# New assignment of heads to groups, column-half loads of wq and wk, and a new instruction order in a transformer block on one core

## The chip, the cores and the metric

The kernel runs on one core of a Trainium2 chip. The metric is the device time of one execution in microseconds, of which the median of several runs is taken. Five engines run their own instruction streams and meet at semaphores: TensorE (PE in the profile, its weight loads PEld), VectorE (DVE), ScalarE (ACT), GpSimd (POOL) and SyncE (SP). SP here does nothing but issue DMAs.

## The reference

x is 2048 tokens of 640 numbers (bf16). The block computes

```
h   = x + A(layernorm(x))          # attention with a memory, 32 heads of 20
out = h + B(layernorm(h))          # MLP, 640 -> 1728 -> 640, silu
```

A splits the 2048 tokens into four segments of 512. In each segment and for each head it computes

```
p     = softmax(q k^T * scale + causal mask);   a_dot = p v
a_mem = (phi(q) M) / (phi(q) z + 1e-6)          # M, z: from the segments before
o     = g * a_mem + (1 - g) * a_dot             # g = sigmoid(beta) of the head
M    += phi(k)^T v;   z += sum phi(k)           # phi(t) = t + 1 if t > 0, else exp(t)
```

and multiplies the concatenated heads with wo. wq, wk, wv and wo are 640 by 640, w1 is 640 by 1728 and w2 1728 by 640.

## The kernel before, in words

**Tiles and stages.** Each 128-token block goes through layer norm (task `n1_st` statistics, `n1_rs` reciprocal root on POOL, `n1_ap` application), is transposed and becomes the moving operand of the projections. The first four blocks are transposed on TensorE against an identity (`n1_tp`, L791) and copied out (`n1_te`, L800); later ones by a DMA (`n1_tr`, L806). Statistics of blocks 1 and 2 can run on ACT (L744 to L748) or on DVE (L753, L756).

**Heads.** 32 heads of 20 numbers form eight groups of four. q and k of a segment live in five chunks of 128 partitions. In a chunk each of four row blocks of 32 partitions holds 20 numbers of one head of a whole group, and in its last 12 partitions a part of a head of one of the remaining three groups: chunks 0 to 2 hold 12 numbers of the heads of groups 5 to 7, chunks 3 and 4 the other 8 of groups 5 and 6 and 4 plus 4 of group 7. `rearr` (L687 to L717) copies the raw weights, which lie in `wraw` (a part of the tile sT), into that order: tasks `re_wq0`, `re_wq0h` (chunk 0 in two parts by rows), `re_wq1` to `re_wq4`, and the same for wk. Groups 5 to 7 get their q and k in one piece through 12 small SBUF-to-SBUF DMAs for each segment, `vt<segment><0..11>` (L908), issued by SP.

**One tick** is a head group in a segment: scores q k (`qk`, L946, four row tiles of the array), exp on ACT (`e`, L959, two pieces for each of the score blocks a, b and, for every second group, e), causal mask on POOL (`mk`, L971), p v (`av`, L994, four column tiles), scaling (`oe`), transposition back and memory part (`td`, `tm`), division and sum (`nm`, `ad`). Ticks 0 to 7 belong to segment 0, 8 to 15 to segment 1 and so on. After a segment come the memory sums (`kt` transposes phi(k) by DMA, `mz`, L1112, multiplies it with v), wo, the second layer norm and the MLP (`h1`, `th`, `s`, `h2`, then `o` and the store `out`).

**Order.** Nothing is scheduled at run time. `ORDER` (L362) is a list of 1462 task names made beforehand, with each task's buffer slots and, where there is a choice, the engine (/A ACT, /D DVE, /G POOL, /S SP). `/C` has a full 128-column matmul issued as four matmuls on column tiles of 32 (L549 instead of L548). The emission follows the list, so each engine executes its tasks in list order, and a wait holds up all that stands behind it on that engine. PE thus changes between three tilings of its array: full (L548, L620, L791), four row tiles (L946) and four column tiles (L549, L994, L1112, L1198).

**Loads at the start.** SP issues, in this order, x block 0, block 1, blocks 2 and 3 together, wq in two parts by rows of the input dimension (480 and 320 KB), wk likewise, wv, beta, x blocks 4 to 7, then parts of w1. The two parts of wq follow `KS`, the two row ranges:

```
KS = [range(0, 3), range(3, 5)]
load_w(f"{n_}{z}", wraw[:, w_, k0_:k1_, :], cw(src)[:, k0_:k1_, :], ...)      # 1280-byte runs
```

In the list the first projections are `pr000x`, `pr000y`, `pr001x`, `pr001y` (chunk 0, q and k, two 256-token halves each), then `pr011`, and after it the first scores `qk0a0`.

Of the kernel before, what the change touches and what calls it, by code (L numbers as in the profile page):

```python
# [234 lines left out]
class Graph:  # L235
# [52 lines left out]
    def schedule(self):  # L288
# [3 lines left out]
        for row in ORDER:  # L292
# [53 lines left out]
GRP_BLK = [[(0, 0)], [(1, 2)], [(2, 4)], [(3, 6)], [(4, 9)],  # L346
           [(0, 1), (3, 7)], [(1, 3), (4, 10)], [(2, 5), (3, 8), (4, 11)]]
# [25 lines left out]
pr041.0:2 e1b0:6 pr041.1 x8/S:8,9,10,11 v03.1 e1b2 qe041/D:0 ex031:0 qk2a0:4,6 n1_tr4 mm5 mk0e pa041:2 n1_rs6 n1_ap6:2
n1_tr6 n1_ap7:3 ex041:2 mzc10 mm2 mk0b pr040.0:3 e2a0:3 mta3 pr040.1 pr030.0:2 ve03/D e2a2 qk2b0:4,0 e2b0:0 vt06
pr030.1/C qe040/D pa031:0 av0:3 pb021 mk1a qe030/D mm1 n1_tr7 vt05 oe0/D:0 qk2e0:6,4 vt010 mk1b av1:2 e2b2 epsg1 mk2b
pb041 mk2a td0/C:3 e2e2:5 e2e0 oe1/D:1 qk3a0:4,0 nm0:3,0 vt07 e3a2:6 v10.0:2 td1:6 nm1:2 vt011 e3a0 v10.1 ve10/D:1
qk3b0:0,6 e3b2:4 e3b0 mm7 n1_st9:2 mk2e av2:3 mk3a oe2/D:1 qk4a0:6,4 e4a2:3 v11.0/C:2 e4a0 v11.1/C qk4b0:0,4 td2/C:6
epsg0 ve11/D pb031 mk3b nm2:2 mtb3 av3:7 e4b0:1 vt01 e4b2 vt02 n1_rs9 oe3/D:0 mzc1 n1_st10:7 vt08 n1_st8:1 vt04
qk4e0:2,0 mk4a pr100.0/C:4 e4e2:4 pr100.1/C qe100/D:0 pa100:0 qk5a0:0,6 pr110.0/C:5 pr110.1/C e4e0 qe110/D:0 e5a0:5
w_wo/S:0 qk5b0:2,0 pr120.0/C:4 pr120.1/C qe120/D:0 mk4b e5a2 mk4e av4:5 oe4/D:1 mk5a kt02:0 pa120:0 e5b2:2 qk6a0:0,6  # L380
n1_rs8 td3/C:4 n1_ap8:0 nm3:0 e5b0 mk5b v12.0:2 v12.1 kt04:4 ve12/D e6a0:1 ex120:0 e6a2 w_w2_3/S td4:1 ex100:1 mz01:0
mz00 mm8 mz04 mz02 kt03:1 n1_rs10 n1_ap10:3 mz03 ma0/D:0 qk6b0:4,2 e6b2:0 e6b0 mk6b nm4:3 pr101.0:7 pr101.1 qk6e0:0,2
e6e2:6 qe101/D av5:6 pr111.0/C:7 pr111.1/C e6e0 qk7a0:4,2 mk6e w_w2_0/S mk6a e7a0:4 e7a2 n1_tr8:1 mk7a oe5/D:0 qe111/D
td5:6 pr130.0/C:0 pr130.1/C nm5:1 n1_tr10 qk7b0:6,4 e7b2:5 e7b0 mk7b n1_ap9:0 qe130/D:0 n1_st11:7 v13.0:1 mm3 v13.1/C
ve13/D ex101:2 n1_rs11 av6:0 qk8a0:3,6 e8a0:3 pa101:0 e8a2 pr140.0:5 pr140.1/C av7:4 oe6/D:1 mzc3 qk8b0:0,2 w_w1_4/S
td6/C:6 e8b0:2 w_w1_3/S n1_tr9 mzc5 pb101 kt10:1 qe140/D:0 oe7/D:0 mk8a nm6:2 pr131.0/C:7 td7/C:4 nm7:1 mzc7 mzc4
ot0:0 qk8e0:5,0 pr131.1/C ot1 n1_ap11:1 mm0 qe131/D pr121.0:4 pr121.1 pa130:0 pa110:0 ot2 qe121/D vt19:0 pa131:1 mzc0
# [935 lines left out]
```

## Time and profile before

| | us |
|---|---|
| median of 3 runs (297.17 to 298.87) | 297.37 |
| the profiled execution, its own time | 295.65 |
| its span in the trace | 293.9 |
| PE busy | 282.0 |
| DVE busy | 218.6 |
| ACT busy | 216.5 |
| POOL busy | 148.1 |

The profiled execution took 295.65 us, 1.75 us more than the span between its first and last recorded instruction, and 1.72 us less than the median of the three runs. Busy time of PE is modelled from pipelined matmuls, so a busy PE is not PE at its peak. In timelines the columns are start, duration, engine, line, operation, output and input, count, and in brackets the idle time before with what ended it. SPq marks the time that SP's DMA queue took to issue.

### The profile page before, as it was taken

Reading aid. Unit: us, or ns where it says so; the run is one execution under the profiler, and the core shown is the slowest. Engines: PE = TensorE matmul, PEld = TensorE weight load, DVE = VectorE, ACT = ScalarE, POOL = GpSimd, SP = SyncE. Lnnn points to the kernel's source line nnn. Section 1 sums busy time; section 2 is a strip of 40 time slices with the busy share of each in tenths; the row PEclk is TensorE's granted clock in tenths of the full one; section 3 lists DMA queues with packets and bytes.
Section 4 is the critical chain, followed back from the end, with each engine's and each line's share of the span. In section 5 each row is a group of like instructions: output and inputs, shape, how many; then the busy total and the mean of one; then the engine's idle time right before and its main releaser. Section 6 shows DMA issues by size and latency. Waiting matters only on the chain.

```text
span 293.9 us, 10138 instructions
## 1 busy us (share of the span) xinstructions
PE 282.0 (96%) x4365; PEld 159.8 (54%) x4365; DVE 218.6 (74%) x456; ACT 216.5 (74%) x281; POOL 148.1 (50%) x294
## 2 busy tenths in 40 slices
PE   6899889999999999999999899999999999999996
PEld 5454435445644445566654554656664657754574
DVE  3999888899997678798899835877746776635613
ACT  7699999999999899977789857979979640005400
POOL 6759675686947545746748432348638321300000
PEclk9999999999999999999999999999999999999999
DMA  7947869635464200453543402403320031450003
GB/s 212 342 120 186 113 176 186 167 69 108 87 80 113 73 2 3 53 99 70 91 122 92 93 2 21 81 2 57 73 25 2 2 70 22 91 156 0 3 0 112
DMA packets 48604, 24.83 MB, mean 84 GB/s; under 512 B 38896, under 2 KB 47472, under 8 KB 48560
## 3 DMA queue, kind: packets, MB, share of 16 engines
q1 hardware_dynamic: 48560, 24.19, 38.1%
q8 instruction: 34, 0.56, 0.8%
q14 instruction: 10, 0.08, 0.1%
HBM read 10.41 MB, written 2.62 MB: 44 GB/s over the span
## 4 chain that ended last, share of the span: by engine, by line
PE 83%; DVE 7%; ACT 6%; DMA 1%; issue 1%; POOL 0%; SPq 0%; ACTq 0%; DVEq 0%
PE ps_all L548 49%; PE ps_all L549 20%; PE ps_all L946 8%; ACT PT L959 5%; PE ps_all L994 5%; DMA x_tok<-in_A_x_dram 1%; PE ps_all L1198 1%; DVE xn_rot L781 1%; DVE oTs L1010 1%; DVE phiQ L890 1%; DVE stt L753 1%; PE ps_all L1112 1%; DVE Vx L843 1%; DVE otok L1046 1%; DVE QK L877 0%
## 5 line engine op out<-in xcount | busy, mean ns | idle before, releaser
L959 ACT ACTIVATE PT<-ps_all 128x1024 bf16<-128x1024 f32 x160 | 154.1, 1027 | 16.2 <-PE ps_all L946 15.1
L971 POOL TENSOR_SCALAR_AFFINE_SELECT PT<-PT 128x512 bf16<-128x512 bf16 x128 | 82.8, 651 | 63.9 <-ACT PT L959 60.5
L1211 ACT ACTIVATE th<-ps_all 128x512 f32<-128x512 f32 (+1 forms) x56 | 31.7, 589 | 38.1 <-PE ps_all L548 23.7
L1217 DVE SCALAR_TENSOR_TENSOR sT<-th,ps_all 128x512 bf16<-128x512 f32 (+1 forms) x56 | 36.0, 661 | 17.0 <-ACT th L1211 16.4
L548 PE MATMUL ps_all<-w_sb,sT 128*128 128x320 bf16 x324 | 46.3, 299 | 0.1
L548 PE MATMUL ps_all<-tT,w_sb 128*128 128x512 bf16 x178 | 41.4, 380 | 0.0
L548 PEld LDWEIGHTS ps_all<-w_sb,sT 128*128 128x128 bf16 x324 | 31.0, 98 | 13.2 <-issue 0.6
L753 DVE BATCH_NORM_STATS2 stt<-x_tok 128x6 f32<-128x320 bf16 x62 | 27.1, 478 | 3.8 <-DMA x_tok<-in_A_x_dram 3.6
L1072 POOL TENSOR_TENSOR otok<-on 128x320 bf16<-128x320 bf16 x24 | 19.7, 824 | 17.5 <-DVE on L1064 17.5
L1254 DVE SCALAR_TENSOR_TENSOR x_tok<-ps_all,x_tok 128x640 bf16<-128x640 f32 (+1 forms) x17 | 13.3, 784 | 17.9 <-PE ps_all L548 13.1
L548 PEld LDWEIGHTS ps_all<-tT,w_sb 128*128 128x128 bf16 x178 | 16.5, 98 | 18.7 <-issue 0.6
L877 DVE CAST QK<-ps_all 128x512 bf16<-128x512 f32 x25 | 17.1, 685 | 8.6 <-PE ps_all L548 4.7
L1010 DVE TENSOR_SCALAR oTs<-ps_all,lsc 128x512 bf16<-128x512 f32 x26 | 19.3, 741 | 2.6 <-PE ps_all L994 2.2
L549 PE MATMUL ps_all<-tT,w_sb 128*32 128x512 bf16 x328 | 20.5, 380 | 0.0
L1064 DVE TENSOR_TENSOR on<-ps_all,rd 128x640 bf16<-128x640 f32 x24 | 19.8, 824 | 0.8
L765 POOL TENSOR_TENSOR rst<-rst,eps_c 128x1 f32<-128x1 f32 x32 | 18.3, 573 | 2.5
L549 PE MATMUL ps_all<-w_sb,sT 128*32 128x320 bf16 x496 | 18.8, 300 | 0.0
L781 DVE TENSOR_SCALAR xn_rot<-x_tok,mvt,rst 128x640 bf16<-128x640 bf16 x31 | 16.1, 534 | 3.3 <-POOL rst L765 2.8
L548 PE MATMUL ps_all<-tT,wkr 128*128 128x512 bf16 (+1 forms) x77 | 18.4, 367 | 0.0
L548 PE MATMUL ps_all<-wv_sb,tT 128*128 128x320 bf16 x115 | 18.0, 300 | 0.5 <-ACT PT L959 0.3
L763 POOL TENSOR_TENSOR rst<-mvt,eps_c 128x1 f32<-128x1 f32 x32 | 6.7, 209 | 22.5 <-DVE mvt L756 21.8
L994 PE MATMUL ps_all<-PT,Vx 128*32 128x512 bf16 (+3 forms) x384 | 17.4, 301 | 0.0
(111 smaller groups left out, 403.1 us busy)
## 6 DMA issues: line engine op xcount, KB each, us to landing
out_dram<-x_tok SPq DMA_DIRECT2D x15, 160.0 KB, 1.9
w_sb<-in_B_w_dram SPq DMA_DIRECT2D x5, 432.0 KB, 4.1
x_tok<-in_A_x_dram SPq DMA_DIRECT2D x3, 640.0 KB, 4.4
w_sb<-in_B_w_dram SPq DMA_DIRECT2D x3, 480.0 KB, 4.0
QKV<-QK SPq DMA_DIRECT2D x12, 72.0 KB
wv_sb<-in_A_wv_dram SPq DMA_DIRECT2D x1, 800.0 KB, 8.2
wo_sb<-in_A_wo_dram SPq DMA_DIRECT2D x1, 800.0 KB, 5.3
w_sb<-in_B_w_dram SPq DMA_DIRECT2D x1, 640.0 KB, 6.0
```

The lines of the kernel that those rows point to most:

```text
L548: return [lambda e: e.matmul(out, lhsT=lhsT, rhs=rhs, start=start, stop=stop)]
L549: return [lambda e, p=p: e.matmul(out[p:p + 32, :], lhsT=lhsT[:, p:p + 32], rhs=rhs, start=start, stop=stop, tile_position=(0, p)) for p i ...
L753: T.add(DV, lambda e, hh=hh: e.bn_stats(out=stt[:, s, 6 * hh:6 * hh + 6], in_=xb[:, 320 * hh:320 * hh + 320]), reads=R((xa, xsub)), writes ...
L946: fns.append(lambda e, j=j, o=o, r=r, q0=q0, q1=q1, qa=qa, ka=ka: e.matmul(ps_all[:, o:o + q1 - q0], lhsT=ka[32 * r:32 * r + DH, 128 * j:1 ...
L959: T.add(AC, lambda e: e.activation(out=pt[:, pta.slot, q0:q0 + 2, 0:width], in_=sc3[:, b0:b0 + 2, 0:width], func=ACT.Exp, scale=SCALE), re ...
L971: fns.append(lambda e, v=v: e.affine_select(out=v, in_=v, pattern=[[0, 4], [1, 128]], compare_op=ALU.is_ge, fill=0.0, base=0, channel_mult ...
L994: fns.append(lambda e, j=j, r=r, h=h, pa=pa, pt=pt, co=co, q0=q0, ji=ji: e.matmul(bank(po)[32 * r:32 * r + 32, q0:hi], lhsT=vtile(vx)[:, j ...
L1010: f = lambda e: e.tensor_scalar(out=o, in0=i_, scalar1=lsc[:, g:g + 1], scalar2=None, op0=ALU.mult)
L1064: T.add(DV, lambda e: e.tensor_tensor(out=on[:, ona.slot, :, :].rearrange("p b (x e) -> p b x e", e=DH), in0=v[:, :, :, 0:DH], in1=r2.unsq ...
L1072: T.add(PO, lambda e: e.tensor_tensor(out=o_dst, in0=on[:, ona.slot, 0, :].rearrange("p (i x) -> p i x", i=4), in1=on[:, ona.slot, 1, :].r ...
L1211: T.add(AC, lambda e: e.activation(out=th[:, tha.slot, lo:hi], in_=bank(ps)[:, lo:hi], func=ACT.Tanh, scale=0.5), reads=R((ps, [0])), writ ...
L1217: T.add(DV, lambda e: e.scalar_tensor_tensor(out=sT[:, f, lo:hi], in0=th[:, tha.slot, lo:hi], scalar=1.0, in1=bank(ps)[:, lo:hi], op0=ALU. ...
```

## The change

It has four parts.

1. **Heads.** A table `SG = [0, 2, 6, 4, 5, 1, 3, 7]` says which four consecutive heads make up each group. Chunk 0 now holds heads of the weights' blocks 0 and 1, chunk 1 of blocks 2 and 3, which all lie in columns 0 to 319. Chunk 2 needs columns 320 to 639 alone, chunks 3 and 4 both halves.
2. **Loads.** wq and wk are loaded in column halves of 400 KB, in the order q left, k left, q right, k right.
3. **Memory sums.** Chunks 3 and 4 swap their parts of groups 5 and 6 (`GRP_BLK`, `blk_type`). `mz` of chunk 4 now is one run of three heads with a constant stride, 16 matmuls of 63 columns, instead of 16 of 42 and 16 of 21 columns.
4. **A new list**: other order, slots and engines for the same 1462 names.

```
+SG = [0, 2, 6, 4, 5, 1, 3, 7]
...
-        for z, ks in enumerate(KS):
-            k0_, k1_ = ks[0], ks[-1] + 1
-            load_w(f"{n_}{z}", wraw[:, w_, k0_:k1_, :], cw(src)[:, k0_:k1_, :], -94 + w_, 6.58, [(sT0, [f"{n_}{z}"])], "fix",
+        for z in range(2):
+            load_w(f"{n_}{z}", wraw[:, w_, :, 320 * z:320 * z + 320], cw(src)[:, :, 320 * z:320 * z + 320], -94 + 2 * z + w_, 6.58,
...
+        four = lambda g: hv[:, :, 4 * SG[g]:4 * SG[g] + 4, :]
...
+            parts = sorted({SG[g] // 4 for g in [c] + ([5 + c] if c < 3 else [2 + c, 7])})
...
-                rr, ww = [(sT0, ["qk"[wi] + q for q in ("01" if c else "01"[z])])], [(W[k], [c + 5 * z])]
+                rr, ww = [(sT0, [f"{'qk'[wi]}{q}" for q in parts])], [(W[k], [c + 5 * z])]
...
-                heads = [(4 * c, 16, 2)] if c < 3 else [(12, 8, 3)] if c == 3 else [(16, 8, 2), (28, 1, 1)]
+                heads = [(4 * SG[c], 4, 2)] if c < 3 else [(4, 12, 3)] if c == 3 else [(12, 8, 3)]
```

The list up to the second half of the first score block, before and after:

```
-epsc:0 iota halfc zpad warm:0 x0:0 mt2 n1_st0:4 mt3 mt0 mt1 mta1 mtb1 vpad1 x1:1 n1_st1/A:1,2 x2:2,3 w_q0:0 w_q1 w_k0
-vpad0 fill25:0 n1_rs0 n1_ap0/A:1 sel n1_tp0:2 fill5:7 n1_te0/A:1 n1_st2/D:5,3 mta0 n1_rs1 n1_st3:0 n1_rs2 w_k1 w_wv:0
-n1_rs3 re_wk4/G:0 mtb0 mm4 n1_ap1 n1_tp1:0 n1_ap2 n1_tp2:4 n1_ap3:0 n1_tp3:2 re_wq0/D:0 n1_te1/A pr000x.0:6 re_wq0h/D
-re_wk2/G pr000x.1 re_wk0/D re_wq2/D n1_te2/A n1_te3/A pr001x.0:5 qe000x/D:0 re_wk0h/D pr000y.0:4 re_wq3/G beta
-pr001y.0:0 x4/S:4,5,6,7 pr000y.1 qe000y/A w_w1_1/S:0 mta2 mtb2 mm10 pr001y.1 re_wk1/D re_wq1/D qe001y/A pr001x.1
-pr011.0:2 pr011.1 re_wk3/D qe001x/A re_wq4/G qk0a0:0,3 ex001:0 pa001:0 pb001 kt00:2 pr021.0:7 pr021.1 e0a2:4 qe011/D:0
...
+iota:0 halfc mt3 x0:0 zpad fill25:0 sel n1_st0:0 mt1 epsc mta1 mtb1 warm:0 x1:1 n1_st1/D:6,1 x2:2,3 n1_st2/A:4,3
+w_q0:0 w_k0 n1_rs0 n1_rs1 n1_ap0/D:2 n1_st3:7 w_q1 w_k1 n1_ap1 n1_tp0:2 fill5:7 n1_rs2 n1_ap2 n1_te0/A:0 re_wq0/A:0
+n1_tp1:5 re_wq0h/D n1_rs3 w_wv:0 n1_tp2:0 n1_ap3:0 n1_tp3:2 n1_te1/A pr000x.0:4 re_wk0/G:0 re_wk0h/G n1_te3/D n1_te2/A
+re_wq2/A pr000x.1 qe000x/D:0 re_wq1/A re_wk1/D beta mm5 pr001x.0:6 pr001x.1 pr001y.0:1 x4/S:4,5,6,7 pr000y.0:4
+pr000y.1 pr001y.1 re_wk2/D pr011.0:7 pr021.0:3 qe000y/A qe001y/A qe001x/A ex001:2 qk0a0:4,1 pa001:2 pb001 pr021.1
+pr011.1 vpad0 qe021/D:0 pr010.0:6 pr010.1 qe011/D:0 pa011:1 e0a2:1 n1_st4:1 kt00:4 x8/S:8,9,10,11 qk0b0:2,0 e0a0
```

Counted over the whole program, PE has 4365 matmuls before and 4356 after, with the same number of columns, and changes the tiling of its array 173 times before and 177 times after. After the start, PE's order in segment 0 is close to the old one (`qk0b0`, `pr020`, `v00`, `qk0e0`, `v01`, `v02`, `qk1a0`, `pr031`, and so on). Of the choices of engine in segment 0, `qe020` goes from ACT to DVE, `re_wq0`, `re_wq1` and `re_wq2` from DVE to ACT, and one load of w1 (`w_w1_3`) is issued from ACT. In SP's order of segment 0, `n1_tr6` (the last of the four block transposes that segment 1's projections need) stood ahead of all but three of the twelve `vt` issues before; after, it stands behind the last of them.

More of the change, by code (lines that the diff above doesn't have):

```diff
@@ L373 @@
[L373 to L387, printed above, removed]
@@ L673, in build @@
             channel_multiplier=-1), reads=[f"mt{k}"], writes=[f"mt{k}"], prio=1)
[L674 to L675 removed]
+    blk_type = {0: 0, 2: 0, 4: 0, 7: 0, 10: 0, 1: 1, 3: 1, 5: 1, 6: 2, 9: 2, 8: 3, 11: 3}
+    blk_head = {m: 4 * SG[g] for g, bl in enumerate(GRP_BLK) for _, m in bl}
     for k in range(12):
@@ L1007, in e_ot @@
                 if eng == AC:
-                    f = lambda e: e.activation(out=o, in_=i_, func=ACT.Identity, scale=lsc[:, g:g + 1])
+                    f = lambda e: e.activation(out=o, in_=i_, func=ACT.Identity, scale=lsc[:, SG[g]:SG[g] + 1])
                 else:
-                    f = lambda e: e.tensor_scalar(out=o, in0=i_, scalar1=lsc[:, g:g + 1], scalar2=None, op0=ALU.mult)
+                    f = lambda e: e.tensor_scalar(out=o, in0=i_, scalar1=lsc[:, SG[g]:SG[g] + 1], scalar2=None, op0=ALU.mult)
                 T.add(eng, f, reads=R((po, [0]), (C, ["lsc"])), writes=R((ots, [0])))
```

203 lines of the change are left out of this document (108 added, 95 removed).

## Prediction

> **What bounds the kernel now.** I read the page first (shares of the chain that ended last), then windows of ten microseconds, then the timeline of the start, since the change names the start.
>
> ```profile
> PE   6899889999999999999999899999999999999996
> ACT  7699999999999899977789857979979640005400
> PE 83%; DVE 7%; ACT 6%; DMA 1%; issue 1%; POOL 0%; SPq 0%; ACTq 0%; DVEq 0%
> ...
> 0.00:10.00 10.00, 6.40 (x50) 4.55 (x50) 4.89 (x18) 7.22 (x11) 6.51 (x27) 1.00 0.81 257
> ...
> 30.00:40.00 10.00, 8.05 (x186) 4.31 (x178) 7.91 (x19) 9.86 (x12) 6.57 (x14) 1.00 0.65 78
> 40.00:50.00 10.00, 9.02 (x243) 4.78 (x236) 9.34 (x20) 9.44 (x12) 6.88 (x14) 1.00 1.10 249
> 50.00:60.00 10.00, 9.96 (x169) 4.38 (x165) 8.78 (x19) 9.90 (x11) 6.02 (x11) 1.00 0.59 127
> ```
>
> In the windows the columns after the length are PE, PEld, DVE, ACT and POOL. PE carries the chain. It is idle for 10.00 - 6.40 = 3.6 us of the first ten (fillers included in busy), 1.95 us at 30 to 40 and 0.98 us at 40 to 50, where ACT is busy for 9.86 and 9.44 of ten. Of PE's 293.9 - 282.0 = 11.9 us of idle time, 6.5 lie in these three windows. So the start counts in full, segment 0 (to about 60 us) is bound by ACT and PE together, and the rest by PE.
>
> The timeline of the start:
>
> ```profile
> 2.19 1.00 SPq L584 DMA_DIRECT2D sT<-in_A_wq_dram  x2
> 3.24 1.00 SPq L584 DMA_DIRECT2D sT<-in_A_wk_dram  x2
> 3.59 0.74 ACT L744 ACTIVATE xn_rot<-x_tok 128x640 bf16<-128x640 bf16 x1 [0.23 <-DMA x_tok<-in_A_x_dram]
> 5.42 0.19 ACT L748 ACTIVATION_READ_ACCUMULATOR xn_rot<-x_tok,stt 128x1 f32 x1
> 5.88 0.88 DVE L753 BATCH_NORM_STATS2 stt<-x_tok 128x6 f32<-128x320 bf16 x2 [1.56 <-DMA x_tok<-in_A_x_dram]
> 7.07 0.70 ACT L800 ACTIVATE tT<-ps_all 128x640 bf16<-128x640 f32 x1 [0.55 <-PE ps_all L791]
> 7.08 0.19 POOL L763 TENSOR_TENSOR rst<-mvt,eps_c 128x1 f32<-128x1 f32 x1 [0.56 <-DVE mvt L756]
> 7.35 0.55 POOL L765 TENSOR_TENSOR rst<-rst,eps_c 128x1 f32<-128x1 f32 x1
> 9.22 0.45 DVE L781 TENSOR_SCALAR xn_rot<-x_tok,mvt,rst 128x640 bf16<-128x640 bf16 x1 [0.51 <-POOL rst L765]
> 9.73 0.45 PE L791 MATMUL ps_all<-ident,xn_rot 128*128 128x128 bf16 x5 [0.51 <-DVE xn_rot L781]
> 10.08 0.71 PE L548 MATMUL ps_all<-tT,wqr 128*128 128x256 bf16 x5
> 10.45 1.06 POOL L711 COPY wkr<-sT 128x400 bf16<-128x400 bf16 x3 [1.33 <-DMA sT<-in_A_wk_dram]
> 11.86 1.68 PE L548 MATMUL ps_all<-tT,wkr 128*128 128x256 bf16 x9
> 12.06 0.94 ACT L876 ACTIVATE w_sb<-ps_all 128x256 bf16<-128x256 f32 x3 [1.14 <-PE ps_all L548]
> 13.03 0.63 ACT L883 ACTIVATE ex<-w_sb 128x512 bf16<-128x512 bf16 x1
> 13.47 0.39 PE L946 MATMUL ps_all<-w_sb 20*128 20x512 bf16 x4
> 13.80 1.25 PE L548 MATMUL ps_all<-tT,wkr 128*128 128x512 bf16 x5
> 13.92 1.94 ACT L959 ACTIVATE PT<-ps_all 128x1024 bf16<-128x1024 f32 x2 [0.26 <-PE ps_all L946]
> 18.39 0.60 ACT L876 ACTIVATE w_sb<-ps_all 128x512 bf16<-128x512 f32 x1
> ```
>
> What the reader is to see: only POOL ever waits for the weights (until 10.45, for wk). PE's first projection at 10.08 follows block 3's transpose (9.73), its normalization (9.22), the reciprocal roots on POOL, and the x load that landed at 5.88. The weights are not the gate; the layer norm of blocks 2 and 3 is.
>
> **The change, part by part.** *Layer norm at the start.* The x loads keep their place, so blocks 2 and 3 land at 5.88 again. The new list puts block 2's statistics on ACT. Block 1's took 3.59 to 5.42 + 0.19 = 5.61 there, 2.02 us, so block 2's end at 5.88 + 2.02 = 7.90. The root tasks stand on POOL in the order 2, 3; each takes 7.08 to 7.35 + 0.55, 0.82 us. So block 2's root is done at about 8.75 and block 3's, though its statistics are early, at 9.6. Block 3's normalization (0.45) ends at 10.05 and its transpose (0.45) at 10.55. The first projection starts at about 10.55 instead of 10.08: **+0.45 us** on PE.
>
> *First scores.* The 20 half projections of chunk 0 took 10.08 to about 12.3 (11.86 + 1.68, less 1.25 for the five 512-column ones in that row): 2.2 us, so they now end at 12.75. Ahead of the first scores now stand six 512-column matmuls (`pr011.0`, `pr021.0`) at 0.24 each (1.25 / 5), as against five: 14.2 instead of 13.47. The first exp comes about 0.75 later, at 14.65. ACT itself is ready by then: from 7.90 it does three copies (0.70 each), the half `re_wq0` and two whole rearrangements, which no row shows on ACT. By the 0.63 and 0.94 / 3 rows for 512 and 256 numbers I put 0.55 and 0.85 for them; that gives 12.3, then 0.94 and 0.63, 14.1. The slack is half a microsecond.
>
> *ACT after that.* `qe020` (0.60, the row at 18.39) goes to DVE, which loses five rearrangements at the start. A load of w1 is issued from ACT, and no row shows that; on SP the two issues of a weight part take 1.00 together, so between 0 and 0.5 for one. ACT's stream is thus between 0.75 - 0.60 = +0.15 and +0.65 late, PE's 0.45 late. I take **+0.45** for both, with ends of 0 (the list is otherwise close to the old one, and idle time of PE at 30 to 50 can take it up) and +1.0.
>
> *The loads.* Half of each weight is enough for chunk 0. wk's last part was issued at about 3.75 and landed at about 10.4 (POOL's row). The bytes ahead of each part are known: 655 KB of x, then 410 KB each. If time goes by bytes, k left lands at about 8, q right at 9.2 and k right at 10.4. Needed: q left at 8.6, k left at 9.6 (POOL), q right at 10.6 (ACT), k right at about 12.3 (DVE). All are hidden, so the loads gain **0**: POOL's wait of 1.33 goes, and what is late next on the path is the root of block 3. If the cover were gone, each microsecond would delay the first scores by one.
>
> The runs shrink from 1280 to 640 bytes, 1280 packets more. Their price is bounded by these rows, of 3 to 11 us and of 292 to 294 us:
>
> ```profile
> DMA packets 2155, 2.64 MB, mean 330 GB/s; under 512 B 94, under 2 KB 2155, under 8 KB 2155
> q1 hardware_dynamic: 2155, 2.64, 102.2%
> ...
> DMA packets 288, 0.16 MB, mean 82 GB/s; under 512 B 32, under 2 KB 288, under 8 KB 288
> q1 hardware_dynamic: 288, 0.16, 26.4%
> ```
>
> At the start a packet of about 1225 bytes takes 16 x 8 x 1.022 / 2155 = 61 ns. At the end, stores of 640-byte rows take 16 x 2 x 0.264 / 288 = 29 ns. So half a packet costs about half, and I take 0; the upper end is a full 61 ns each, rival 3. The Trainium skill, "DMA: Bandwidth & Descriptors", Why small descriptors are slow, gives a packet about 3 cycles beside its 32-byte beats, by which 640 bytes cost 46 cycles for what took 43: as an estimate k right would land some 0.3 us later, still hidden. The same page's Specifications put the limit for line rate at 512 bytes. The trace's 29 ns agree with both, and rival 3 gets 5 rather than 10 in 100 for it.
>
> *Tilings of PE.* PE changes between full, row-tiled and column-tiled matmuls 177 times instead of 173. The price, from equal columns with and without a change:
>
> ```profile
> 55.45 0.85 PE L548 MATMUL ps_all<-wv_sb,tT 128*128 128x320 bf16 x5
> 56.23 0.86 PE L549 MATMUL ps_all<-wv_sb,tT 128*32 128x320 bf16 x20
> 56.92 0.71 PE L994 MATMUL ps_all<-PT,sT 128*32 128x512 bf16 x16
> ...
> 95.14 0.82 PE L1112 MATMUL ps_all<-Vx,phiKt 128*32 128x42 bf16 x80
> 95.79 0.84 PE L549 MATMUL ps_all<-tT,wqr 128*32 128x512 bf16 x12
> ```
>
> The five full ones hold PE until the column-tiled ones start, 0.78 us; the 20 column-tiled ones of the same columns, with no change after them, 0.69. So a change costs about 0.1, and four cost **+0.4**, ends 0 (covered by ACT's exps) and 0.5. The Trainium skill, "TensorEngine Tiling (Array Packing)", Key Properties, says that changing the tiling mode drains TensorE, which speaks against the new list; "TensorE: Matmul & The Clock Gate" has about 166 ns as the constant of an isolated warm matmul, by which, as an estimate, four would cost 0.66. The row's 0.1 decides.
>
> *Memory sums.* 16 matmuls fewer in each of three segments, with the same columns. 80 took 95.79 - 95.14 = 0.65 us, 8 ns each, so 48 save at most 0.4; if columns alone count, 0. I take **-0.2**. The rest of the list has the same work on each engine; where it creates or closes a wait I can't see one by one, and take 0, with the rivals as ends.
>
> The sum is 0.45 + 0.4 - 0.2 = +0.65. Against the profiled execution's own 295.65 that is 296.3. The median of the runs stands 1.72 above it, and on that basis I predict 297.37 + 0.65 = **298.0 us**.
>
> **Rivals.** *1, the start pays as it is meant to.* If block 2's statistics or ACT's copies go faster than the rows, or ACT bounds segment 0 alone and only its 0.60 less counts: -0.6 to -1.1, PE's idle 2.9 us at 30 to 50 shrinking with it. With the +0.2 of the other terms: about 296.7. For it speaks ACT's 9.86 of ten; against it, that block 3's root stands behind block 2's on POOL.
>
> *2, SP's queue in segment 0 (slower).* Segment 1's first projection needs all four block transposes, and `n1_tr6` is now behind the last `vt`.
>
> ```profile
> 30.01 2.45 SPq L806 DMA_TRANSPOSE tT<-xn_rot  x1
> 32.51 5.64 SPq L908 DMA_DIRECT2D QKV<-w_sb  x8
> ...
> 30.16 0.69 DVE L877 CAST w_sb<-ps_all 128x512 bf16<-128x512 f32 x1
> ...
> tT<-xn_rot SPq DMA_TRANSPOSE x28, 2.7
> ...
> 41.17 1.26 PE L549 MATMUL ps_all<-tT,wqr 128*32 128x512 bf16 x20 [0.52 <-ACT PT L959]
> ```
>
> The nine `vt` left start when chunk 3's q is copied, 30.85 + 0.45 = 31.3. At 0.70 each they end at 37.7, and a landing 2.7 later, 40.4, is in time for 41.6 (41.17 + 0.45). If the transpose's issue takes 2.45, as at 30.01, and the `vt` 0.85 each, it lands at 43: PE waits 1.4 us, with `qk5a` and `qk6a` behind it, and ACT runs out of scores. That gives 299.4. It decides from a landing later than 41.6; the same pattern in a later segment would double it to 300.8.
>
> *3, small packets (slower).* At 61 ns for each packet of 640 bytes the 1280 more take 1280 x 61 / 16 = 4.9 us: k right lands at 15.3 instead of 10.4. `re_wk2` on DVE and `pr021.0` on PE wait for it, the first scores come at about 16.4, exp 2.9 later than before; less 0.60, plus 0.2: 299.9.
>
> **How the numbers follow.** Chances: the forecast 0.48, rival 1 0.22, rival 2 0.25, rival 3 0.05. The likeliest one's own range is 297.0 to 299.0. The range for 8 in 10 reaches from below rival 1's (296.7, less another 0.9 for PE waits that close and for the low profiled run) to beyond rival 2's 299.4 and 3's 299.9: 295.8 to 300.6. A measurement of this kernel can tell about 1% from no change, 3.0 us. Faster than 294.4 needs rival 1 with most of the idle 2.9 us on top: 0.08. Slower than 300.3 needs rival 2 twice, or 2 and 3: 0.17. Within: 0.75.
>
> **What would show it.** In the changed kernel's timeline: the first L551 matmul (L548 before) at 10.5 rather than 10.1, behind POOL's root of block 3; no engine waiting for wq or wk; the first exp at about 14.6; `n1_tr6` landing before segment 1's first projection. I am wrong if PE starts before 10.0, if DVE or ACT waits for a weight DMA, or if PE shows new waits of a microsecond after 60 us.

## The result, and the profile after

The changed kernel takes 302.0 us (median of 6 runs, 300.68 to 305.92) against 298.12 us for the kernel before beside it: a ratio of 1.0144, with a 95% interval of 1.0097 to 1.0192. Measured again in a later set (run 5 below) it is 301.47 against 296.61, 1.0172 (1.0122 to 1.0221). The prediction was 298.0, with a range up to 300.6: the change is slower, where no change that can be measured was forecast. The profiled execution took 301.97 us, its span is 300.2. Medians are of all runs; ratios leave out runs more than 1.5% above the fastest of their kernel.

The start took the path that was predicted. The timeline of the changed kernel, as shown for the one before (line numbers are three higher here: L551 is L548):

```profile
5.47 0.74 ACT L747 ACTIVATE xn_rot<-x_tok 128x640 bf16<-128x640 bf16 x1 [2.10 <-DMA x_tok<-in_A_x_dram]
...
7.57 0.19 POOL L766 TENSOR_TENSOR rst<-mvt,eps_c 128x1 f32<-128x1 f32 x1 [1.07 <-ACT xn_rot L751]
8.35 0.19 POOL L766 TENSOR_TENSOR rst<-mvt,eps_c 128x1 f32<-128x1 f32 x1
9.45 0.45 DVE L784 TENSOR_SCALAR xn_rot<-x_tok,mvt,rst 128x640 bf16<-128x640 bf16 x1 [0.31 <-POOL rst L768]
9.96 0.45 PE L794 MATMUL ps_all<-ident,xn_rot 128*128 128x128 bf16 x5 [0.51 <-DVE xn_rot L784]
10.25 0.71 PE L551 MATMUL ps_all<-tT,wqr 128*128 128x256 bf16 x5
13.90 0.40 PE L949 MATMUL ps_all<-w_sb 20*128 20x512 bf16 x4
14.34 1.02 ACT L962 ACTIVATE PT<-ps_all 128x1024 bf16<-128x1024 f32 x1 [0.26 <-PE ps_all L949]
```

Block 2's statistics on ACT hold the two roots on POOL, the first projection comes at 10.25 (0.17 us later than before) and the first exp 0.42 us later. In this execution `x_tok` landed 0.41 us earlier than in the profile before; in the second profile of the same kernel (run 5) it landed at 5.78, and the first projection came at 10.56, the first exp 0.74 us later. POOL's copies of wk, which waited 1.33 us for a load before, show no wait now. By tick 5 the exps are 0.13 us behind the kernel before (0.71 in run 5). The larger loss comes later. The windows of ten microseconds (columns as before), first the changed kernel, then the kernel before:

```profile
80.00:90.00 10.00, 8.12 (x100) 3.94 (x101) 7.90 (x16) 6.92 (x10) 5.88 (x10) 1.00 0.66 92
90.00:100.00 10.00, 9.47 (x156) 4.47 (x158) 6.87 (x14) 9.19 (x13) 5.30 (x8) 1.00 0.55 128
150.00:160.00 10.00, 9.27 (x177) 5.00 (x176) 6.81 (x14) 8.15 (x11) 3.30 (x6) 1.00 0.72 145
```

```profile
80.00:90.00 10.00, 10.00 (x135) 5.04 (x134) 8.75 (x18) 9.52 (x14) 5.96 (x10) 1.00 0.61 107
90.00:100.00 10.00, 9.87 (x250) 4.83 (x251) 7.98 (x16) 9.05 (x13) 6.20 (x12) 1.00 0.38 98
150.00:160.00 10.00, 10.00 (x194) 4.64 (x186) 9.41 (x20) 9.90 (x14) 5.55 (x12) 1.00 0.38 97
```

PE is idle for 1.88 us where it had been busy throughout (80 to 90). These are joints: the end of a segment's attention, where the memory sums, wo, the second layer norm and the first MLP matmuls meet the next ticks. What PE waited for after 60 us (total, times, longest), changed kernel and then the kernel before:

```profile
PE ps_all L551 <- issue: 1.6, 1, 1.6
PE ps_all L552 <- issue: 1.3, 2, 0.7
PE ps_all L551 <- DMA tT<-xn_rot: 1.1, 2, 0.6
PE ps_all L949 <- DVE sT L1220: 0.5, 1, 0.5
...
PE ps_all L551 <- DMA tT<-otok: 0.4, 1, 0.4
```

```profile
PE ps_all L946 <- issue: 0.9, 1, 0.9
PE ps_all L548 <- ACT PT L959: 0.3, 1, 0.3
PE ps_all L548 <- DVE x_tok L1176: 0.3, 1, 0.3
PE ps_all L946 <- DVE otok L1046: 0.2, 1, 0.2
```

PE's waits after 60 us have grown from 1.7 to some 6 us in this execution (4.4 in the profile of run 5), and of the larger ones some name a DMA or, as shown below, hide one. Over the whole span PE's idle time grew from 11.9 to 15.7 us, and its busy time by 2.5 us, of which 1.2 are the filler matmuls of the start. In the chain that ended last (section 4 of the page) PE had 83% before, DVE 7% and DMA 1%; in the changed kernel:

```profile
PE 58%; DVE 21%; ACT 7%; DMA 6%; issue 4%; POOL 2%; SPq 2%; POOLq 0%; DVEq 0%; ACTq 0%
```

DVE's share grew more than that of DMA. The shares do not measure the loss: the kernel of run 1 below, which loses nothing, has PE 72%, DVE 12%, DMA 5%.

The largest wait, 1.59 us (0.70 in run 5), is that of `h1_0_0_0`, the first MLP matmul. SP's queue ahead of it, in the changed kernel and in the one before (SPq is SP's queue of issues, with start and duration of each group; L809, L806 are the layer norm's transposes, L911, L908 the `vt`, L1104, L1101 the `kt`):

```profile
69.05 3.60 SPq L809 DMA_TRANSPOSE tT<-xn_rot  x2
72.69 2.97 SPq L911 DMA_DIRECT2D QKV<-QK  x4
75.71 1.21 SPq L1104 DMA_TRANSPOSE phiKt<-phiK  x1
76.96 2.12 SPq L911 DMA_DIRECT2D QKV<-QK  x2
79.12 6.78 SPq L809 DMA_TRANSPOSE tT<-xn_rot  x4
85.95 1.27 SPq L1104 DMA_TRANSPOSE phiKt<-phiK  x1
87.26 3.54 SPq L911 DMA_DIRECT2D QKV<-QK  x5
```

```profile
69.51 1.28 SPq L806 DMA_TRANSPOSE tT<-xn_rot  x1
70.83 5.12 SPq L908 DMA_DIRECT2D QKV<-QK  x7
76.00 6.59 SPq L806 DMA_TRANSPOSE tT<-xn_rot  x4
82.64 0.65 SPq L908 DMA_DIRECT2D QKV<-QK  x1
83.33 1.19 SPq L1101 DMA_TRANSPOSE phiKt<-phiK  x1
```

SP issues without a pause from 69 to 91 us; before, it did so too, up to 86. The four `n2_tr` go out at 79.12 to 85.90 instead of 76.00 to 82.59, because `n1_tr10` (20 us earlier before) and `kt11` (behind them before) now stand ahead. PE starts at 87.57, 1.67 us after the last issue ended. The last `n2_tr` landed at 87.27 by the trace, 0.30 us before PE started (run 5: 86.18 and 86.48), so the wait that the profile calls issue is that transpose's landing.

**Theory 1**, from here: the list is the cause, by SP's order at the joints. **Theory 2**: the 640-byte packets or the column halves. **Theory 3**: the heads, memory sums and tiling changes.

### The profile page after: what moved, and what is told of

It reads as the page before. It is cut to its first block, busy times and chain, and to the rows that moved or that the text cites. A ratio compares the mean times of both kernels' runs of the same rounds, so it can differ in the third digit from the quotient of the medians.

```text
span 300.2 us, 10109 instructions
## 1 busy us (share of the span) xinstructions
PE 284.5 (95%) x4356; PEld 159.4 (53%) x4356; DVE 218.4 (73%) x450; ACT 215.0 (72%) x282; POOL 148.5 (49%) x299
## 4 chain that ended last, share of the span: by engine, by line
PE 58%; DVE 21%; ACT 7%; DMA 6%; issue 4%; POOL 2%; SPq 2%; POOLq 0%; DVEq 0%; ACTq 0%
PE ps_all L551 29%; PE ps_all L552 18%; PE ps_all L949 6%; ACT PT L962 4%; PE ps_all L997 4%; DMA tT<-xn_rot 4%; DVE stt L756 3%; DVE xn_rot L784 3%; DVE x_tok L1179 2%; DVE sT L1220 2%; ACT th L1214 2%; DMA tT<-otok 1%; POOL rst L768 1%; DMA x_tok<-in_A_x_dram 1%; DVE otok L1049 1%
## 5 line engine op out<-in xcount | busy, mean ns | idle before, releaser
L551 PE MATMUL ps_all<-tT,w_sb 128*128 128x512 bf16 x203 | 47.5, 379 | 2.2 <-issue 1.6
L551 PE MATMUL ps_all<-w_sb,sT 128*128 128x320 bf16 x324 | 46.0, 299 | 0.1
L551 PEld LDWEIGHTS ps_all<-w_sb,sT 128*128 128x128 bf16 x324 | 31.2, 98 | 12.9 <-ACT oTs L1011 0.4
L551 PEld LDWEIGHTS ps_all<-tT,w_sb 128*128 128x128 bf16 x203 | 18.5, 98 | 24.0 <-issue 3.9
L1257 DVE SCALAR_TENSOR_TENSOR x_tok<-ps_all,x_tok 128x640 bf16<-128x640 f32 (+1 forms) x17 | 13.2, 782 | 15.2 <-PE ps_all L551 14.1
L886 ACT ACTIVATE ex<-QK 128x512 bf16<-128x512 bf16 x25 | 15.6, 635 | 3.0 <-DVE QK L880 3.0
L949 PE MATMUL ps_all<-QK 20*128 20x512 bf16 (+3 forms) x240 | 15.1, 301 | 0.8 <-DVE sT L1220 0.5
L552 PE MATMUL ps_all<-tT,w_sb 128*32 128x512 bf16 x228 | 14.5, 380 | 0.7 <-issue 0.7
```

Source lines behind the costliest of these rows:

```text
L551: return [lambda e: e.matmul(out, lhsT=lhsT, rhs=rhs, start=start, stop=stop)]
L552: return [lambda e, p=p: e.matmul(out[p:p + 32, :], lhsT=lhsT[:, p:p + 32], rhs=rhs, start=start, stop=stop, tile_position=(0, p)) for p i ...
L949: fns.append(lambda e, j=j, o=o, r=r, q0=q0, q1=q1, qa=qa, ka=ka: e.matmul(ps_all[:, o:o + q1 - q0], lhsT=ka[32 * r:32 * r + DH, 128 * j:1 ...
```

## Experiments

The five sets had the kernel before beside them at 297.11, 296.61, 296.73, 297.45 and 296.61 us. Each ratio is to it, with its 95% interval.

### 1 and 2: code and list exchanged

The changed code with the old list (`mm6`, `mm7` and so on renamed with their blocks):

```
 ORDER = """
-iota:0 halfc mt3 x0:0 zpad fill25:0 sel n1_st0:0 mt1 epsc mta1 mtb1 warm:0 x1:1 n1_st1/D:6,1 x2:2,3 n1_st2/A:4,3
...
+epsc:0 iota halfc zpad warm:0 x0:0 mt2 n1_st0:4 mt3 mt0 mt1 mta1 mtb1 vpad1 x1:1 n1_st1/A:1,2 x2:2,3 w_q0:0 w_q1 w_k0
...
```

> The changed kernel's heads, column-half loads and memory sums with the list of the kernel before (its order, slots and engines; four pairs of mask names are renamed with the blocks that changed places). Theory 1 (the loss is the new list's order on SP's queue at the joints of segments): no such wait is left, so -0.2 us for the memory sums, between -0.8 and +0.4 against the kernel before. Theory 2 (the 640-byte packets or the column halves): +3 to +5 us, and PE's first work after the start later. Theory 3 (heads and tiling changes): the list of before has its own 173 tiling changes again, so the heads alone would have to cost +1 us or more. In the trace theory 1 has the first MLP matmul of segment 0 at 84.4 us, as before, with the last transpose of the second layer norm issued by 82.6.

Measured: 295.39 us, 0.9938 (0.9906 to 0.9970). The heads, loads and memory sums cost nothing; with the old list they gain 1.7 us, more than expected. The first MLP matmul came at 85.74, not at the expected 84.4, though the last transpose was issued by 82.64. The old code with the new list is the same exchange the other way:

> The converse: heads, row-part loads and memory sums of the kernel before, with the new list. Theory 1: the whole loss is there, +4.3 us against the kernel before, and with the row parts at the start (the half of chunk 0 now waits for wk's second part on POOL until about 10.4) up to 0.8 more: +3.5 to +5.2. Theory 2 and theory 3: within 1 us of the kernel before. In the trace theory 1 has the first MLP matmul of segment 0 at 87.5 us or later, behind the same order of issues on SP.

Measured: 301.28 us, 1.0103 (1.0043 to 1.0163). So the list makes the loss, and neither theory 2 nor theory 3 makes it alone. But code and list do not simply add up: the list costs 6.1 us (medians) to 7.0 us (ratios) with the new code, and 3.1 (ratio) to 4.2 us (medians) with the old; the new code gains 1.7 us with the old list and nothing that can be measured with the new one. Why is open.

### 3 and 4: three and five issues moved within the stretch

SP's tasks in list order:

```
-vt18 vt10 vt17 vt19 kt11 vt13 vt16 n2_tr0 n2_tr2 n2_tr1 n2_tr3 kt13 vt15 vt111 vt14 vt12 vt11
+vt10 vt19 vt13 vt16 n2_tr0 n2_tr2 n2_tr1 n2_tr3 vt18 vt17 kt11 kt13 vt15 vt111 vt14 vt12 vt11
```

> The changed kernel, with three issues on SP (vt18, vt17 and kt11, 0.69 + 0.64 + 1.21 = 2.54 us) put behind n2_tr3, the last transpose of the second layer norm in segment 0, instead of ahead of the first. Theory 1: the transposes go out 2.5 us earlier, the last one at 83.3 instead of 85.9; the first MLP matmul comes at about 85.1 instead of 87.6, and the time falls by about 2.5 us (1.5 to 3.0) against the changed kernel, so it is +1.8 against the kernel before. A rival (the wait there only takes up time that PE would lose later): less than 0.5 us, with the wait found again behind tick 13. Theory 2 and 3: no change.

Measured: 304.16 us, 1.0192 (1.0128 to 1.0256): no gain. In its profile PE's wait at the first MLP matmul is gone, and this one has come (84 to 96 us):

```profile
PE ps_all L947 <- issue: 2.4, 1, 2.4
```

It is the third score block of tick 12, whose second matmul reads what the `vt` write. The last of them, `vt11`, was issued by 89.97, and PE went on at 91.77. In the changed kernel the same block goes on at 92.60, also 1.80 us after the last `vt` was issued (90.80). So the block followed that issue, which came only 0.83 us earlier: an exchange within a full queue moved the wait. The fourth run also moved two `kt` in segment 2:

```
-n2_tr4 vt28 n2_tr5 kt20 kt21 out1 n2_tr7 n2_tr6
+n2_tr4 vt28 n2_tr5 out1 n2_tr7 n2_tr6 kt20 kt21
```

> As the run before, and in the next segment kt20 and kt21 (1.25 us each) behind n2_tr6, the last transpose there, instead of ahead of n2_tr7. Theory 1: PE's waits at h1_1_1_0 (0.73 us) and at the two matmuls that follow it go; another -0.7 us (0 to -1.2), so about +1.1 us against the kernel before. The rival: nothing more than the run before.

Measured: 303.95 us, 1.0253 (1.0195 to 1.0312). In segment 2 SP is not full: the two transposes wait for their normalizations on DVE.

### 5 and 6: the changed kernel again, and issues taken out of the stretch

> The changed kernel unaltered, as the comparator for the three runs beside it. All theories: +1.0 to +1.9% against the kernel before, about 301.5 us.

Measured: 301.47 us, 1.0172 (1.0122 to 1.0221). Beside it:

```
-n1_tr8 kt10 ot0 ot1 ot2 ot3 vt110 w_w1_4 n1_tr10 n1_tr11 vt18 vt10 vt17 vt19 kt11 vt13 vt16 n2_tr0 ... n2_tr3 kt13 vt15 ... vt11
+n1_tr8 n1_tr10 w_w1_4 kt10 ot0 ot1 ot2 ot3 vt110 n1_tr11 vt18 vt10 vt17 vt19 vt13 vt16 n2_tr0 ... n2_tr3 vt15 ... vt11 kt11 kt13
```

> The changed kernel with four issues taken out of the full stretch of SP's queue in segment 1 (69 to 91 us): n1_tr10 and the w1 load w_w1_4 go right behind n1_tr8, into a stretch (51 to 60 us) in which SP has nothing to issue, and kt11 and kt13 go behind vt11, the last copy that the third score block of tick 12 needs. Theory 1, made sharper by the two runs before (what PE loses at the joint is the time at which SP has done all that is due by tick 12, so that an exchange within the stretch gains nothing): 2.28 + 0.44 = 2.7 us less ahead of the last transpose and 2.28 + 0.44 + 1.21 + 1.27 = 5.2 us less ahead of vt11, which then goes out at about 85.6 instead of 90.8. PE's 1.59 and 0.53 us at the joint go, tick 13 starts about 2.5 us earlier, and the time falls by 2.5 us (1.5 to 4) against the changed kernel. Rival (PE then waits for another engine at the same joint, DVE's n2_ap or the unexplained issue waits): less than 1 us.

`n1_ap10`, the normalization that `n1_tr10` needs, also goes ahead in DVE's order.

Measured: 302.89 us, 1.0189 (1.0137 to 1.0240). The edit made a wait of its own: `pa121` needs the slot of phiK that `kt11` frees, and DVE stood for it (80 to 100 us), with PE behind.

```profile
DVE phiK L891 <- DMA phiKt<-phiK: 2.9, 1, 2.9
```

### 7 and 11: SP's burden put into the old list

Run 7 moves two issues in the kernel of run 1:

```
-n1_tr8 n1_tr10 ... ot3 n1_tr11 ... vt18 n2_tr1 n2_tr2 n2_tr3 n2_tr0 vt110 kt11
+n1_tr8 ... ot3 n1_tr10 n1_tr11 ... vt18 kt11 n2_tr1 n2_tr2 n2_tr3 n2_tr0 vt110
```

> The converse, on the faster kernel with the list of before and the new heads and loads: n1_tr10 is issued behind ot3 instead of some 20 us earlier, and kt11 ahead of n2_tr1 instead of behind n2_tr0: 1.2 to 2.3 + 1.2 us more on SP ahead of the second layer norm's transposes. Theory 1: the first MLP matmul of segment 0 and tick 13 come 2 to 3.5 us later, and the time is 1.5 to 3.5 us above that kernel's 295.4, so about 297.5 to 298.5. Rivals (heads, loads, tiling): the same time as that kernel, 295.4.

Measured: 298.01 us, 1.0030 (1.0000 to 1.0061), 2.6 above run 1, as theory 1 said. Here the profile names the wait (L549 of this code is L551):

```profile
86.67 2.32 PE L549 MATMUL ps_all<-tT,w_sb 128*128 128x512 bf16 x5 [1.61 <-DMA tT<-xn_rot]
```

Run 11 takes the new SP order of segment 1 as a whole into the old list; all other engines keep the old order:

```
-ot2 vt19 w_w2_4 vt12 ot3 n1_tr11 vt16 vt10 vt13 vt11 vt15 vt14 vt18 n2_tr1 n2_tr2 n2_tr3 n2_tr0 vt110 kt11 vt111 vt17
+ot2 ot3 vt110 w_w1_4 n1_tr10 n1_tr11 vt18 vt10 vt17 vt19 kt11 vt13 vt16 n2_tr0 n2_tr2 n2_tr1 n2_tr3 kt13 vt15 vt111 vt14 vt12 vt11
```

> The converse: the kernel with the list of before and the new heads and loads, with SP's order of segment 1 alone taken from the changed kernel (n1_tr10 late, kt11 and the vt issues ahead of or behind the transposes as there). Theory 1: +1.5 to +3 us above that kernel's 295.4. Rival: within 0.5 of it.

Measured: 299.47 us, 1.0082 (1.0050 to 1.0113), 4.1 above run 1. The order of one queue, in one segment, is worth more than all that the prediction summed. Not all of it need be a price of the order in the changed kernel: SP's new order begins with `n2_tr0`, which DVE in the old order normalizes last, and SP stood 1.2 us for it (78.43 to 79.66).

### 9 and 10: a better order, and the old one, in the new list

```
+n1_tr8 n1_tr10 w_w1_4 kt10 ot0 ot1 ot2 ot3 vt110 n1_tr11 vt18 vt10 vt17 vt19 vt13 vt16 kt11 vt15 vt111 n2_tr0 n2_tr2 vt14 n2_tr1 n2_tr3 vt12 vt11 kt13
```

> The changed kernel with SP's stretch from 66 to 91 us put in the order of the times at which its issues are due: n1_tr10 and w_w1_4 go into SP's empty stretch at 51 us, kt11 stays ahead of pa121 (which needs its slot), two vt and kt11 stand ahead of the second layer norm's transposes, where SP would wait for their normalization, the last vt and kt13 behind them. In the run with kt11 behind the last vt, pa121 on DVE waited 2.86 us for it, and PE behind that; here it doesn't. Theory 1: the last transpose goes out 1.3 us earlier and the last vt 4.5 us earlier; PE's 0.70 and 0.53 us at the joint go, so -1.2 us (0.7 to 2) against the changed kernel. Rival (another engine holds the joint): 0.

`n1_ap10` again goes ahead on DVE too.

Measured: 302.15 us, 1.0167 (1.0121 to 1.0213): no gain is seen, but the difference to the changed kernel is known to some 2 us only, so the expected 1.2 us are neither shown nor excluded. Run 10 gives SP the old order in segments 0 and 1, other engines as in the changed kernel:

```
-n1_tr9 w_w2_0 w_w1_1 n1_tr8 kt10 ot0 ot1 ot2 ot3
+n1_tr8 n1_tr10 w_w1_4 n1_tr9 kt10 ot0 ot1 ot2 vt19 w_w2_4 vt12 ot3
```

> The changed kernel with nothing but SP's own order altered, in segments 0 and 1: SP issues its DMAs there in the order of the kernel before, while PE, ACT, DVE and POOL keep the changed kernel's order, slots and choices. Theory 1 (SP's order is the cause at this joint): -1.2 to -2.5 us against the changed kernel, with tick 13 that much earlier and the rest of the loss (segments 2 and 3) still there. Rival (the order of the other engines): 0 to -0.5.

Measured: 319.62 us, 1.0755 (1.0700 to 1.0810), the wrong way by 18. SP's `n1_tr10` now stands early, but DVE still does its normalization late (55 to 100 us):

```profile
SPq L807 <- DVE phiQ L897: 18.0, 1, 18.0
```

Behind it wait `n1_tr9`, `kt10` and the `ot`, which had nothing to do with it. Some 10 us more were lost already in segment 0: between the first exps of ticks 4 and 5, where DVE waited 7.8 us for a `kt`. An order of SP is good or bad only against the orders of the others.

### 8, 12 and 18: where the heads gain

Run 8 has run 1's kernel with loads by rows again:

```
-        for z in range(2):
-            load_w(f"{n_}{z}", wraw[:, w_, :, 320 * z:320 * z + 320], cw(src)[:, :, 320 * z:320 * z + 320], ...
+        for z, ks in enumerate(KS):
+            load_w(f"{n_}{z}", wraw[:, w_, k0_:k1_, :], cw(src)[:, k0_:k1_, :], ...
```

> The list of before and the new heads, but wq and wk loaded in parts by rows again (1280-byte runs, chunk 0 waiting for both parts as before). If the column halves were the 1.7 us by which the new heads on the old list beat the kernel before, this is at the kernel before's time, about 297; if the halves neither gain nor cost (the prediction's term), it is at 295.4 like the kernel with halves. Theory 2 (small runs cost) would put it below 295.

Measured: 295.57 us, 0.9979 (0.9949 to 1.0009), run 1's time. Run 12 keeps the halves and issues k left before q right:

```
-w_q0:0 w_q1 w_k0
+w_q0:0 w_k0 w_q1
```

> The list of before, new heads and column halves, with the loads in the order q left, k left, q right, k right (k left issued one place earlier), as the changed kernel has it: what the halves are for. If the start is held by the layer norm of blocks 2 and 3 (the prediction), PE's first projection stays at 10.1 to 10.3 us and the time at 295.4 +- 0.3. If the weights hold it (rival 1), -0.5 to -1.1 us.

Measured: 294.61 us, 0.9947 (0.9919 to 0.9975), the lowest median of the study, but its interval overlaps run 1's. Run 18 splits run 1's memory sums:

```
-heads = [(4 * SG[c], 4, 2)] if c < 3 else [(4, 12, 3)] if c == 3 else [(12, 8, 3)]
+heads = [(4 * SG[c], 4, 2)] if c < 3 else [(4, 12, 3)] if c == 3 else [(12, 8, 2), (28, 1, 1)]
```

> The list of before with the new heads and loads (295.4), with the memory sums of chunk 4 split again into 16 matmuls of 42 and 16 of 21 columns in each segment, 48 matmuls more. If they are what the new heads gain: 296.4, the kernel before's time. The prediction's term of 0.2 us: 295.6. If the gain is elsewhere (the layout of the heads): 295.4.

Measured: 296.38 us, 0.9991 (0.9967 to 1.0015). So 48 small matmuls cost about 1.0 us by the medians, 1.6 by the ratios, whose intervals just touch.

### 13 to 16: the two lists cut and joined

The new list up to a task and the old list's remaining tasks behind it, or the reverse (a slot is changed where its own is taken).

```
+ORDER = new[: new.index("qk14a0")] + [t for t in old if t not in new[: new.index("qk14a0")]]
```

> The changed kernel's heads, loads and code, with the new list up to tick 14 (start, segment 0 and the joint of segment 1) and the list of before for the rest. If the loss lies at the joint alone: about 301, the changed kernel's time. If it is spread as the profiles' starts of ticks say (about 2 of 6 us up to tick 14): 297 to 298. If the joint costs nothing in the new list: 295.4 to 296.

Measured: 299.01 us, 1.0032 (0.9999 to 1.0066).

> The converse: the list of before up to tick 14, the new list for the rest. If the loss lies at the joint alone: 295.4. If it is spread: 299 (298 to 300), and the two losses together make the whole one of 6 us.

Measured: 299.15 us, 1.0047 (1.0019 to 1.0076).

> The new list up to tick 24 (with the joint of segment 2), the list of before for segment 3 and the end. Spread: 299.5 (298.5 to 300.5); the remaining 1.5 to 2 us are then those of segment 3 and the end. At the joint of segment 1 alone: the same as with the cut at tick 14.

Measured: 300.96 us, 1.0123 (1.0071 to 1.0174).

> The list of before for the start and segment 0 (to tick 8), the new list for the rest. The profiles put 0.5 to 1.0 us of the loss into the start and segment 0, so 300.5 to 301; if the new start and segment 0 pay, the time is above the changed kernel's 301.5, if they carry more, it is below 300.

Measured: 300.23 us, 1.0098 (1.0066 to 1.0130).

Differences of ratios times 297 us, from run 1 (0.9938) to the changed kernel (1.0172): to tick 14 it is 2.8 us (run 13), from 14 to 24 another 2.7 (run 15), the rest 1.5; runs 13 and 15 came out slower than was expected of a spread loss (297 to 298 and 298.5 to 300.5). The other way round: the beginning up to tick 8 is 2.2 (run 16), ticks 8 to 14 are 1.5 (run 14 against 16), all behind them 3.2. Each has some 1 to 1.5 us of uncertainty, and a joined list may have waits of its own at the seam, which was not tried apart. The loss is spread; the joint of segment 1 is a part of it, not the whole.

The profiled runs say the same. How much later than in the kernel before one and the same exp of a tick (its first piece of score block a) starts on ACT, and how much later the last store starts, in us:

| task (start before) | changed | again (5) | old list (1) | run 9 | run 11 | 13 | 14 | 16 |
|---|---|---|---|---|---|---|---|---|
| tick 8 (58.06) | 0.48 | 1.06 | -0.09 | 2.27 | -0.04 | 2.90 | -0.68 | -0.50 |
| tick 12 (83.72) | 1.17 | 0.97 | 1.11 | 2.17 | 0.47 | 2.81 | 0.15 | 0.47 |
| tick 13 (92.60) | 3.84 | 2.74 | 1.33 | 3.68 | 5.29 | 4.95 | 0.31 | 2.29 |
| tick 18 (122.32) | 3.40 | 2.30 | 1.19 | 3.25 | 5.15 | 4.80 | -0.04 | 1.85 |
| tick 22 (155.87) | 5.25 | 3.29 | 1.20 | 4.61 | 5.16 | 4.81 | 2.15 | 4.44 |
| last store (291.85) | 6.30 | 4.81 | 0.51 | 6.84 | 3.86 | 3.84 | 2.81 | 4.96 |

From tick 12 to 13 the new order costs 2.7, 1.8 and, mended, 1.5 us; in the old list 0.2 (run 1). From 18 to 22 it costs 1.0 to 2.6.

### 17: PE kept busy in the wait

```
 td10:6 e12a0 tm10
+fill24:2
 h1_0_0_0.0:2
```

> The kernel with the new order of SP's segment 1 in the old list (299.5 us, clock below full in 9 of 10 runs), with 24 matmuls of 256 columns on a zero tile put on PE ahead of the first MLP matmul, where PE waited 3.73 us for the transposes; their result is overwritten, so only time is added: 24 x 0.11 = 2.6 us, inside the wait. If the clock falls because PE is idle: no row with a granted clock under 0.95 at 86 to 92 us, and 297.5 us (297 to 298), 2 us faster for more work. If the clock's fall has another cause: 299.5 or more.

Measured: 298.92 us, 1.0077 (1.0046 to 1.0107), against 299.47 in run 11. The windows of both at the joint, run 11 first (the clock is the third number from the end):

```profile
84.00:86.00 2.00, 0.58 (x9) 0.36 (x8) 1.90 (x7) 1.69 (x3) 0.29 (x2) 1.00 0.53 103
86.00:88.00 2.00, 0.00 (x0) 0.00 (x0) 1.09 (x2) 0.00 (x0) 0.65 (x1) 1.00 0.97 146
88.00:90.00 2.00, 1.37 (x4) 0.58 (x5) 0.00 (x0) 0.00 (x0) 0.00 (x0) 0.53 0.08 17
90.00:92.00 2.00, 2.00 (x30) 0.69 (x32) 0.80 (x2) 1.43 (x2) 0.00 (x0) 0.62 0.25 41
```

```profile
84.00:86.00 2.00, 2.00 (x21) 1.79 (x20) 1.67 (x4) 0.63 (x2) 0.79 (x1) 1.00 1.57 77
86.00:88.00 2.00, 0.47 (x5) 0.17 (x2) 0.00 (x0) 0.00 (x0) 0.00 (x0) 1.00 0.79 63
88.00:90.00 2.00, 1.26 (x9) 0.51 (x13) 0.00 (x0) 0.00 (x0) 0.00 (x0) 1.00 0.33 51
```

With the matmuls the clock stays at 1.00; its mean over the run was below full (0.994 or less) in 1 of 9 runs, against 9 of 10 in run 11. So the fall is a price of the idle PE. But the gain was 0.5 us instead of 2, within the uncertainty: PE still waited 2.27 us behind them for the transposes, and the first exp of tick 13 came 4.31 us later than in the kernel before, that of tick 12 0.59 earlier: 4.9 us lost at the joint, as in run 11 (5.29 - 0.47 = 4.8). The trace shows where the half clock's time went. The last transpose's issue ended 1.7 us earlier than in run 11 (84.27 against 85.99), but it landed later (88.43 against 87.94), so PE started at 88.74 against 88.63. Behind the wait, up to the third score block, run 17 then took 3.88 us against 4.99: 1.1 us came back. Why the landing took so long is open.

## Why the prediction was wrong

**The start, +0.45: right on the path,** and in size where `x_tok` landed about as before (5.78 against 5.88): +0.75 was forecast for the first exp, and run 5's profile has +0.74, its first projection 10.56 against the forecast 10.55. The first profile has +0.42 and 10.25, with `x_tok` 0.41 us earlier than in the kernel before. One sum of the prediction is off: ACT is ready at 12.3 + 0.94 + 0.63 = 13.87, not 14.1, so it had 0.8 us of room; nothing came of that, as the first exp waited 0.26 us for PE. But the cut at tick 8 puts 2.2 us into the start and segment 0. The profiles of the changed kernel show 0.5 to 1.1 there. In five of nine profiled kernels with that beginning (run 10 aside) the clock falls inside it, as in run 13, where the kernel before had 1.00 with PE busy for 8.05:

```profile
30.00:40.00 10.00, 7.58 (x146) 3.37 (x144) 9.41 (x19) 8.11 (x10) 6.94 (x14) 0.83 0.33 62
```

0.83 over ten microseconds is 3.4 us at half speed. The runs of these nine kernels had a mean clock below full in 30 of 60, those of runs 1, 8, 12, 14, 16 and 18, which begin with the old list, in 5 of 72; a fall anywhere in the run counts there. In run 13 two of the runs below full took 299.49 and 300.57 us, the nine others 298.31 in the median: 1.7 us, what 3.4 us at half speed lose. In run 5, from which the 2.2 are taken, 1 of 6 runs was below full, so the clock explains some 0.3 of them. With the profiles' 0.5 to 1.1 that makes 0.8 to 1.4 us against 2.2, a difference within the uncertainty. What in the new beginning thins PE out was not tried alone.

**The loads, 0: right.** Halves or rows (run 8) and either order of the halves (run 12) give the same time, within the uncertainty. Rival 3 falls by run 8. Rival 1 falls by the profiles: at the end of segment 0 the changed kernel is not earlier but 0.48 and 1.06 us later.

**Memory sums, -0.2: right in sign, too small.** They measured -1.0 to -1.6 (run 18). The price of 8 ns for one was taken as a bound for what 48 can save; it was no bound. With the old list this is nearly all that the new code gains.

**Tilings, +0.4: not measured by themselves.** Run 1 has the old list's 173 changes, so it says nothing on the four more.

**The rest of the list, 0: this step failed.** "The rest of the list has the same work on each engine; where it creates or closes a wait I can't see one by one, and take 0, with the rivals as ends." Equal work on each engine says nothing of the order in which queues meet. The list's term measured +6 to +7 us (runs 1 and 5, with what the list does at the start and the tilings in it; 3 to 4 us with the old code, run 2), and it turned the sign: without it the change gains 0.6%. Part of it is shown to lie in SP's queue at the joint of segment 1; what makes the rest is open. The order of DVE in the new list, whose share of the chain grew from 7 to 21%, was not tried by itself, nor were the list's other choices of engine and slot.

**Rival 2 had the mechanism, and looked for it in the wrong place.** It allowed for the pattern in a later segment, at 300.8 us, and its sign, new waits of PE of a microsecond after 60 us, came true (1.59 us; 0.70 in run 5). `n1_tr6`, behind nine `vt`, held nobody. The same pattern, transposes behind `vt` and `kt` on SP, held PE at the joint of segment 1, where SP issues for 22 us without a pause. The prediction looked for it in segment 0, because it followed SP's order only there; counting SP's issues between 66 and 91 us in both lists would have shown `n1_tr10` and `kt11` ahead of the `n2_tr`.

**Theory 1 of the experiments was right on what the queue can cost** (runs 7 and 11 put it in and lost 2.6 and 4.1 us) **and wrong as the whole cause.** It predicted gains of 2.5, 2.5 and 1.2 us from runs 3, 6 and 9, and none was seen; the comparisons are good to some 2 us. Runs 3 and 6 show a wait in another place of the same joint. The cut lists show that other parts of the new list lose too, in segment 2 and at the end, by waits of about a microsecond or less (run 14 behind tick 14: 1.0, 0.8, 0.8 and 0.5 us for the largest).

The version to keep is the new heads and loads with the old list (run 1, 0.9938, or run 12, 0.9947): some 0.6% faster than the kernel before, with intervals that exclude 1, and 2% faster than the changed one.

## What to carry over

When an order of issues is exchanged, count for each queue what stands ahead of each thing that is due, at every joint, and not only where the change says it acts; equal work per engine is no argument. To separate a rewritten kernel from its reordered list, exchange the two, and cut the lists at a few tasks before mending anything. A mend in one queue must be held against the slots that its issues free and against the orders of the other engines, or it makes a new wait.

## What the runs showed of the hardware

After a wait or a sparse stretch of PE the granted clock falls to 0.5 for about 3.4 us (runs 7, 11 and 13). The Trainium skill, "TensorE: Matmul & The Clock Gate", Part 1, says that an idle window of about 3.4 us takes TensorE to half rate. Run 11 agrees: PE waits for 3.73 us from 84.90 on, and the clock falls at 88.12; in the 3.4 us before that PE was busy for 0.19. Less idleness did it too: in run 7 PE was busy for 1.60 of the 3.4 us before the fall, in run 13 for 1.64. The windows of run 7, whose wait was 1.61 us:

```profile
84.00:86.00 2.00, 0.75 (x10) 0.36 (x8) 1.93 (x6) 1.85 (x3) 0.32 (x1) 1.00 1.01 97
86.00:88.00 2.00, 1.33 (x4) 0.51 (x5) 1.22 (x3) 0.00 (x0) 0.79 (x1) 0.64 0.33 47
88.00:90.00 2.00, 2.00 (x19) 0.50 (x21) 0.34 (x1) 0.97 (x2) 0.00 (x0) 0.50 0.71 233
```

The issue of one and the same transpose is not constant either: the four `n2_tr` kept SP for 6.78 us in the changed kernel and 6.59 in the one before, 5.8 and 5.2 us in runs 1 and 17. A single one took 1.27 to 2.41 us in the changed kernel and landed 1.4 to 3.1 us after its issue ended; the last one of run 17 landed 4.2 us after.
